# Moving elementwise work of a fast-multiplication MoE kernel: add and clamp in one VectorE operation, weight sums and half of the output accumulation to GpSimd and ScalarE

## The chip, the cores and the metric

The kernel runs on one core of one Trainium2 chip. The metric is the device time of one execution in microseconds (us). The engines are named as the profile names them: PE (TensorE matmul), PEld (its weight loads), DVE (VectorE), ACT (ScalarE), POOL (GpSimd) and SP (SyncE, which here only issues DMAs). All of them run their own instruction streams in order and meet through semaphores.

## The reference

A sparse attention (a window of 16 on either side, and summaries of blocks of 32 keys) gives `x`, 3072 rows of 512. A dense mixture of experts with Sinkhorn weights follows, which is where nearly all of the work lies:

```python
logits = x @ w_gate
P = np.exp(logits - logits.max())
for _ in range(8):
    P /= P.sum(1, keepdims=True) + 1e-09
    P /= P.sum(0, keepdims=True) + 1e-09
    P *= N / E
for e in range(E):                       # E = 8, N = 3072, D = 512, F = 1024
    h = np.maximum(x @ w1[e], 0.0)
    ye = h @ w2[e]
    out += P[:, e:e + 1] * ye
```

## The kernel before

**Stages.** The attention, the gate and all of expert 0 come first. Their units of work are put in order by a planner (class `Plan`), which has costs and dependencies for each unit; its course runs on through the transition (`bridge`), where the eight Sinkhorn steps run on DVE and POOL beside the last products of expert 0 and the first four groups of expert 1. From there on the order is written out by hand, in a loop over n. The last four steps are written out once more (`last`).

**Fast multiplication.** Experts 1 to 7 compute both products in seven block products instead of eight (Strassen's scheme in Winograd's form). Each of them needs sums and differences of blocks of both factors, and of the results. For the first product of a group these are `p1` to `p7`, for the second `q1` to `q7`.

**One iteration** of the loop handles one group (expert e, columns j of 512 rows, part i of the hidden units; 12 groups per expert, i innermost) of the first product, and the pair of output tiles `ta`, `tb` of the group four iterations earlier (LAG = 4) of the second product. PE runs, in this order: q1 (the end of the last line of the iteration before), p1, p5, q5, p6, p2, q6, p3, p7, q2, q4, q3, p4, q7. A p product is two matmuls of 512 columns, a q product four of 256. The other engines, in PSUM banks `pa`, `pb`, `pg` (first product) and `xy` (second product, two buffers of two banks):

- ACT: `r21` (relu of the group before), `c1` (copy of q1's result), `seed` (pa to pg), `c5` and `c2` (copies of pb and pg into SBUF), `r11` (relu), `v6` (a copy inside xy).
- DVE, before: `ya` and `yb` of the pair before (line 1125: out_acc = xy * P + out_acc, 512 elements each), `v5` (xy and c1 into xy, read by q6), `s4` of the group before, then `c12` and `c22` (line 933: pb + c2 and pg + c5 into the f16 tile hf), `r12` and `r22` (lines 1044 and 1047: the clamp at zero, in place), `s1`, `s3`, `s2` (lines 933 and 930: sums of the parts of hf, which the second product reads four iterations later). c22 must be over before p4 adds to the same bank pg, v5 before q6 adds to its part of xy.
- POOL, before: only DMA issues in this part of the kernel: `load_w1` and `load_w2`, which fetch the next expert's weights as f16. One w1 part's load follows each of the first three groups of j = 2, and waits until PE has used the buffer; w2 and the first part of w1 are loaded at j = 1, i = 1.

**Weight sums.** `w1_sums(e, i)` makes three new blocks and overwrites one (four operations of 256 f16 elements); `w2_sum(e, n)` makes one block of 1024 f16 elements. For experts 2 to 7 the loop places w1 parts 0 and 1 at j = 2, i = 2 and 3 of the expert before, w1 parts 2 and 3 at j = 0, i = 0 and 1, the first two w2 sums at j = 2, i = 0 and 1 of the expert before, and the last two at j = 0, i = 2 and 3. Those of expert 1 are in the transition, but for what the planner leaves open.

The lines of the loop that set this order around the change:

```python
            do("q1", "p1")
            do0("r21")
            do("c1", "seed")
            do0("ya", "yb")
            ...
            do("p2", "r11")
            do("q6", "v6")
            do("p3", "c12")
            do("p7", "c22", "r12")
            do("q2", "q4", "q3")
            do("r22", "s1", "s3", "p4", "s2", "q7")
            if groups[n - LAG][0] == 1:
                do("scale0")
```

`do` is for the group and pair of this iteration, `do0` for those of the one before. `scale0` scales expert 0's share of the two output tiles on ACT (line 1081), in expert 1 only. In the last expert each finished tile is stored by SP (line 1129), ta after `ya` and tb after `fin`.

Of the kernel before, what the change touches and what calls it, by code (L numbers as in the profile page):

```python
# [8 lines left out]

FP32 = mybir.dt.float32  # L10
BF16 = mybir.dt.bfloat16
FP16 = mybir.dt.float16
AF = mybir.ActivationFunctionType
ALU = mybir.AluOpType
# [20 lines left out]
class Plan:  # L35
# [13 lines left out]
    def add(self, eng, cost, fn, deps=(), prio=0.0, opens=(), uses=(), lag=0.0, shape=None):  # L49
        u = Unit(eng, cost, fn, [d for d in deps if d is not None], prio, list(opens), lag, shape)  # L50
        for b in list(opens) + list(uses):
            b.users.append(u)
        if uses and eng != "PE":
            u.prio -= 100.0
        self.waiting.append(u)
        return u
# [80 lines left out]
def kernel(  # L137
# [29 lines left out]
    ROW = PAD + HG * (LIVE + PAD) + W + PAD  # L167
    NEH = 3
    XS = 64.0

    const = ctx.enter_context(tc.tile_pool(name="const", bufs=1))
    persist = ctx.enter_context(tc.tile_pool(name="persist", bufs=1))
# [742 lines left out]
    if True:  # L915
# [10 lines left out]
        xTs = fast.tile([128, 3, KH, NH], FP16, name="xTs")  # L926
        ws1, ws2, hs = {}, {}, {}

        def sub(out, in0, in1):
            nc.vector.tensor_tensor(out=out, in0=in0, in1=in1, op=ALU.subtract)  # L930

        def plus(out, in0, in1):
            nc.vector.tensor_tensor(out=out, in0=in0, in1=in1, op=ALU.add)  # L933

        def moving1(what, j):
            t = slice(512 * j, 512 * (j + 1))
# [17 lines left out]
        def w1_sum(e, i, n):  # L954
            if n == 0:
                ws1[e, i] = fast.tile([128, 3, KH, 128], FP16, tag="ws1", name="ws1", bufs=5)
            m = {w: weight1(w, e, i) for w in "A11 A12 A21 A22 S1 S2 S3 S4".split()}
            f, o, a, b = ((plus, "S1", "A21", "A22"), (sub, "S2", "S1", "A11"), (sub, "S3", "A11", "A21"),
                          (sub, "S4", "A12", "S2"))[n]
            f(m[o], m[a], m[b])  # L960

        def w1_sums(e, i):
            for n in range(4):
# [9 lines left out]
        def w2_sum(e, n):  # L973
            if n == 0:
                ws2[e] = hpool.tile([128, 3, FH, DH], FP16, tag="h", name="ws2")
            m = {w: moving2(w, e) for w in "B11 B12 B21 B22 T1 T2 T3 T4".split()}
            sub(*[m[w] for w in (("T1", "B12", "B11"), ("T2", "B22", "T1"), ("T3", "B22", "B12"),
                                 ("T4", "T2", "B21"))[n]])

        def product1(e, i, j, bank, a, b, start):  # L980
            w, x = weight1(a, e, i), moving1(b, j)
# [10 lines left out]
        def group(e, j, i):  # L992
            h = hs[e, j, i] = fast.tile([128, 7, 512], FP16, tag="hf", name="hf", bufs=8)
            B = {}

            def p1():
                B["a"] = fps.tile([128, 512], FP32, tag="ab", name="pa", bufs=2)
                product1(e, i, j, B["a"], "A11", "B11", True)

            def seed():  # L1000
                B["g"] = fps.tile([128, 512], FP32, tag="g", name="pg", bufs=2)
                nc.scalar.copy(out=B["g"][:], in_=B["a"][:])  # L1002

            def p5():
                B["b"] = fps.tile([128, 512], FP32, tag="ab", name="pb", bufs=2)
                product1(e, i, j, B["b"], "S1", "T1", True)

            def c5():
                B["c5"] = fast.tile([128, 512], FP32, tag="c5", name="c5", bufs=1)
                nc.scalar.copy(out=B["c5"][:], in_=B["b"][:])  # L1010

            def p6():
                product1(e, i, j, B["g"], "S2", "T2", False)

            def c2():
                B["c2"] = fast.tile([128, 512], FP32, tag="c2", name="c2", bufs=1)
                nc.scalar.copy(out=B["c2"][:], in_=B["g"][:])  # L1017

            def p2():
                product1(e, i, j, B["a"], "A12", "B21", False)  # L1020

            def r11():
                relu("ACT", h[:, A11, :], B["a"][:])

            def p3():
                product1(e, i, j, B["b"], "S4", "B22", False)

            def c12():
                plus(h[:, A21, :], B["b"][:], B["c2"][:])

            def p7():
                product1(e, i, j, B["g"], "S3", "T3", False)

            def c22():
                plus(h[:, A22, :], B["g"][:], B["c5"][:])

            def p4():
                product1(e, i, j, B["g"], "A22", "T4", False)

            def r21():  # L1040
                relu("ACT", h[:, A12, :], B["g"][:])

            def r12():
                nc.vector.tensor_scalar_max(out=h[:, A21, :], in0=h[:, A21, :], scalar1=0.0)

            def r22():
                nc.vector.tensor_scalar_max(out=h[:, A22, :], in0=h[:, A22, :], scalar1=0.0)

            def s1():
                plus(h[:, S1, :], h[:, A21, :], h[:, A22, :])  # L1050

            def s3():
                sub(h[:, S3, :], h[:, A11, :], h[:, A21, :])

            def s2():
                sub(h[:, S2, :], h[:, S1, :], h[:, A11, :])

            def s4():
                sub(h[:, S4, :], h[:, A12, :], h[:, S2, :])

            return {f.__name__: f for f in (p1, seed, p5, c5, p6, c2, p2, r11, p3, c12, p7, c22, p4,
                                            r21, r12, r22, s1, s3, s2, s4)}

        def pair(e, j, c, spare=False, c1_at=None, tail=False):
            def h(q):
# [55 lines left out]
            def add(t, k, *src):  # L1121
                src = part(*src)
                w = src.shape[1]
                acc = out_acc[:, t, k * DH:(k + w) * DH].rearrange("p (h d) -> p h d", h=w)
                nc.vector.scalar_tensor_tensor(out=acc, in0=src, scalar=P_sb[:, t, e:e + 1], in1=acc,  # L1125
                                               op0=ALU.mult, op1=ALU.add)
# [2 lines left out]
                eng.dma_start(out=out[t * 128:(t + 1) * 128, k], in_=out_acc[:, t, k])  # L1129

            def ya():
                add(ta, 0, 0, 3)
                if e == E - 1:
                    store(ta)

# [34 lines left out]
        def bridge():  # L1170
# [54 lines left out]
            for i in range(4):  # L1225
                f = made[1, 0, i] = group(1, 0, i)
                a, b, g = Buffer("ab"), Buffer("ab"), Buffer("g")
                k5, k2 = Buffer("c5"), Buffer("c2")
                d = {}

                def op(name, eng, us, deps, opens=(), uses=()):
                    d[name] = add(eng, us, f[name], [d[x] if isinstance(x, str) else x for x in deps],
                                  1000.0 + PRI[i], opens=opens, uses=uses)

                op("p1", "PE", 0.44, [U["w1n", i]], [a])
                op("seed", "ACT", 0.58, ["p1"], [g], [a])
                op("p5", "PE", 0.44, ["p1", Wt[i, 0], X[0, 0]], [b])
                op("c5", "ACT", 0.58, ["p5"], [k5], [b])
                op("p2", "PE", 0.44, ["seed"], (), [a])
                op("r11", "ACT", 0.58, ["p2"], (), [a])  # L1240
                op("p6", "PE", 0.44, ["seed", Wt[i, 1], X[0, 1]], (), [g])
                op("c2", "ACT", 0.58, ["p6"], [k2], [g])
                op("p3", "PE", 0.44, ["c5", Wt[i, 3]], (), [b])
                op("c12", "DVE", 0.68, ["p3", "c2"], (), [b, k2])
                op("p7", "PE", 0.44, ["c2", X[0, 2]], (), [g])
                op("c22", "DVE", 0.68, ["p7", "c5"], (), [g, k5])
                op("p4", "PE", 0.44, ["c22", X[0, 3]], (), [g])
                op("r21", "ACT", 0.58, ["p4"], (), [g])
                op("r12", "DVE", 0.3, ["c12"])
                op("r22", "DVE", 0.3, ["c22"])  # L1250
                op("s1", "DVE", 0.42, ["r12", "r22"])
                op("s3", "DVE", 0.42, ["s1", "r11"])
                op("s2", "DVE", 0.42, ["s1"])
                op("s4", "DVE", 0.42, ["s2", "r21"])
# [7 lines left out]
                u.fn()  # L1262
        first.close()
        xps = ctx.enter_context(tc.tile_pool(name="xps", bufs=1, space=PSUM, side="right", reuse_waits="tile"))
        NOTHING = {}
        g = q = NOTHING
        for n in range(LAG, len(groups)):
# [6 lines left out]
            def do(*names):  # L1274
                for nm in names:
                    f = g.get(nm) or q.get(nm)
                    if f is not None:
                        f()

            def do0(*names):  # L1280
                for nm in names:
                    f = g0.get(nm) or q0.get(nm)
                    if f is not None:
                        f()
# [4 lines left out]
            do("q1", "p1")  # L1289
            do0("r21")  # L1290
            do("c1", "seed")
            do0("ya", "yb")
            do("p5", "c5")
            do("q5", "v5")
            do0("s4", "fin")
# [10 lines left out]
                w2_sum(e, i)  # L1306
            do("p2", "r11")
            do("q6", "v6")
            do("p3", "c12")
            do("p7", "c22", "r12")  # L1310
            do("q2", "q4", "q3")
            do("r22", "s1", "s3", "p4", "s2", "q7")
            if groups[n - LAG][0] == 1:
                do("scale0")
            if j == 2 and i < 3 and later:
# [54 lines left out]
```

## Time and profile before

| | |
|---|---|
| median of 3 runs | 669.99 us (669.78 to 670.46) |
| span of the profiled execution | 667.9 us |
| mean granted TensorE clock | 0.999 |
| c12 and c22, 84 times each (DVE) | 692 and 680 ns |
| r12 and r22, 84 times each (DVE) | 284 and 287 ns |
| ya and yb, 164 times together (DVE) | 744 ns |
| s1, s2, s3, s4 (DVE, 512 f16) | 425 ns |
| a copy of 256 or 512 elements from PSUM (ACT) | 372 and 585 ns |
| a scaled copy of 256 elements from PSUM (ACT, line 1152) | 474 ns |
| an f32 operation on two SBUF tensors on POOL: 192 elements (lines 1184 and 1201, medians) | 517 and 592 ns |
| the same, 256 elements (lines 1140 and 1158, in the tail) | 726 and 723 ns |
| a DMA issue of a w1 half part (POOL) | 758 ns |

The result's file has only times of the runs; the profiled execution's own time is not among them, and stands as its span. A busy share is of the span; an idle time that a row shows in brackets is that of the engine just before it, with what ended it. The end of a matmul is modelled, and neighbouring matmuls overlap in the rows.

### The profile page before, as it was taken

What the parts mean: (1) busy time and instruction counts of PE and PEld (TensorE: products, weight loads), DVE (VectorE), ACT (ScalarE), POOL (GpSimd) and SP (SyncE); (2) the same over time, 40 slices, a digit from 0 to 9 for tenths busy, and PEclk for the clock granted to TensorE, in tenths of its full rate; (3) what the DMA queues carried; (4) which work ended last, traced back from release to release, by engine and by line L of the source; (5) the groups of instructions that cost most, each with busy time, mean ns of one, the idle gap of its engine ahead of it and who ended that gap; (6) DMA issues with size and microseconds to landing.
All of it is one profiled execution on the core that took longest, in us unless ns stands there. A gap on an engine that the chain in (4) does not pass through costs nothing.

```text
span 667.9 us, 13518 instructions
## 1 busy us (share of the span) xinstructions
PE 659.0 (99%) x5077; PEld 435.7 (65%) x5077; DVE 582.2 (87%) x1475; ACT 399.7 (60%) x782; POOL 131.8 (20%) x179
## 2 busy tenths in 40 slices
PE   8999999999999999999999999999999999999996
PEld 4766656555666666666666666666666666666665
DVE  8889998785999988998799978998899889998885
ACT  6777676566777765555555555555555555555551
POOL 8699404223011010201010000101020101100001
PEclk9999999999999999999999999999999999999999
DMA  9999939500513050503231051306040233201224
GB/s 162 184 154 147 148 72 95 71 1 8 73 17 32 1 80 1 49 1 55 26 33 17 0 80 17 33 1 79 1 47 3 39 41 29 20 1 64 79 80 158
DMA packets 124033, 36.75 MB, mean 55 GB/s; under 512 B 110144, under 2 KB 121152, under 8 KB 123968
## 3 DMA queue, kind: packets, MB, share of 16 engines
q0 software_dynamic: 104128, 25.93, 41.2%
q1 hardware_dynamic: 18880, 9.22, 6.1%
q8 instruction: 40, 0.66, 0.4%
q10 hardware_dynamic: 960, 0.74, 0.3%
q14 instruction: 25, 0.20, 0.1%
HBM read 52.45 MB, written 6.29 MB: 88 GB/s over the span
## 4 chain that ended last, share of the span: by engine, by line
PE 89%; DVE 7%; DMA 1%; ACT 1%; issue 1%; ACTq 0%; DVEq 0%
PE xy L989 37%; PE pg L983 16%; PE pa L983 11%; PE pb L983 11%; PE yps L231 5%; PE hps L221 5%; DVE xs L547 1%; DMA kT<-kst 1%; PE sg L383 1%; PE tkq L349 1%; DVE em L435 1%; DVE km L377 1%; DVE h L214 0%; DVE kh L375 0%; PE tx L554 0%
## 5 line engine op out<-in xcount | busy, mean ns | idle before, releaser
L989 PEld LDWEIGHTS <-hf 128*128 128x128 f16 x2352 | 230.1, 98 | 95.8 <-issue 0.8
L989 PE MATMUL xy<-w,hf 128*128 128x256 f16 x1312 | 183.4, 273 | 0.0
L989 PE MATMUL xy<-ws,hf 128*128 128x256 f16 x984 | 147.6, 273 | 0.1
L212 ACT ACTIVATE hf<-pg 128x512 f16<-128x512 f32 x84 | 50.1, 597 | 151.3 <-PE pg L983 151.2
L1125 DVE SCALAR_TENSOR_TENSOR out_acc<-xy,P_sb,out_acc 128x512 f32<-128x512 f32 x164 | 115.1, 744 | 2.1 <-PE xy L989 2.1
L930 DVE TENSOR_TENSOR hf<-hf 128x512 f16<-128x512 f16 x252 | 100.3, 425 | 8.9 <-DVE hf L933 0.5
L983 PE MATMUL pa<-xT,w 128*128 128x512 f16 x336 | 99.9, 379 | 0.0
L983 PEld LDWEIGHTS <-w 128*128 128x128 f16 x672 | 65.8, 98 | 43.5
L933 DVE TENSOR_TENSOR hf<-pb,c 128x512 f16<-128x512 f32 x84 | 58.1, 692 | 36.7 <-PE pb L983 34.4
L197 POOL DMA_DIRECT2D w<-in_moe_w_dram x56 | 41.8, 758 | 219.9 <-PE pg L983 191.7
L983 PEld LDWEIGHTS <-ws 128*128 128x128 f16 x504 | 49.3, 98 | 25.1
L1017 ACT COPY c<-pg 128x512 f32<-128x512 f32 x84 | 49.2, 585 | 22.4 <-PE pg L983 22.4
L933 DVE TENSOR_TENSOR hf<-pg,c 128x512 f16<-128x512 f32 x84 | 57.1, 680 | 0.7 <-PE pg L983 0.7
L212 ACT ACTIVATE hf<-pa 128x512 f16<-128x512 f32 x84 | 50.6, 603 | 0.9 <-PE pa L983 0.9
L1002 ACT COPY pg<-pa 128x512 f32<-128x512 f32 x84 | 47.9, 570 | 4.9
L983 PE MATMUL pg<-xT,w 128*128 128x512 f16 x168 | 50.0, 379 | 0.0
L983 PE MATMUL pg<-xTs,w 128*128 128x512 f16 x168 | 50.0, 379 | 0.0
L983 PE MATMUL pb<-xTs,ws 128*128 128x512 f16 x168 | 50.0, 379 | 0.0
L983 PE MATMUL pb<-xT,ws 128*128 128x512 f16 x168 | 50.0, 379 | 0.0
L983 PE MATMUL pg<-xTs,ws 128*128 128x512 f16 x168 | 50.0, 379 | 0.0
L1010 ACT COPY c<-pb 128x512 f32<-128x512 f32 x84 | 49.8, 593 | 0.0
L221 PE MATMUL hps<-xT,w 128*128 128x384 f16 x256 | 48.9, 326 | 0.0
(152 smaller groups left out, 827.5 us busy)
## 6 DMA issues: line engine op xcount, KB each, us to landing
w<-in_moe_w_dram POOLq DMA_DIRECT2D x8, 1024.0 KB, 9.0
w<-in_moe_w_dram POOLq DMA_DIRECT2D x56, 128.0 KB, 3.5
out_dram<-out_acc SPq DMA_DIRECT2D x20, 256.0 KB, 2.0
vx<-in_v_dram POOLq DMA_DIRECT2D x16, 192.0 KB, 5.9
qst<-in_q_dram POOLq DMA_DIRECT2D x31, 96.0 KB, 5.2
kst<-in_k_dram POOLq DMA_DIRECT2D x24, 96.0 KB, 5.4
w<-in_moe_w_dram POOLq DMA_DIRECT2D x2, 512.0 KB, 8.8
Ve<-vx SPq DMA_DIRECT2D x48, 10.2 KB, 4.0
```

The source lines that it names most:

```text
L197: nc.gpsimd.dma_start(out=t[:, :, h, :], in_=moe_w1[e].rearrange("(dk p) f -> p dk f", p=128)[:, :, f:f + 128])
L212: nc.scalar.activation(out=out, in_=in_, func=AF.Relu, bias=0.0, scale=1.0)
L221: nc.tensor.matmul(hp[:, 0:n], lhsT=w1s[e][:, dk, 128 * f:128 * (f + 1)], rhs=xT[:, dk, t0:t0 + n], start=(dk == 0), stop=(dk == KD - 1))
L231: nc.tensor.matmul(yp[:], lhsT=h[:, f, c * 128:(c + 1) * 128], rhs=w2s[e][:, f, :], start=(f == 0), stop=(f == KF - 1))
L930: nc.vector.tensor_tensor(out=out, in0=in0, in1=in1, op=ALU.subtract)
L933: nc.vector.tensor_tensor(out=out, in0=in0, in1=in1, op=ALU.add)
L983: nc.tensor.matmul(bank[:], lhsT=w[:, dk, :], rhs=x[:, dk, :], start=start and dk == 0, stop=dk == KH - 1, skip_group_check=True)
L989: nc.tensor.matmul(bank, lhsT=a(f)[:, 128 * c:128 * (c + 1)], rhs=w[:, f, :], start=start and f == 0, stop=f == FH - 1, skip_group_check=True)
L1002: nc.scalar.copy(out=B["g"][:], in_=B["a"][:])
L1010: nc.scalar.copy(out=B["c5"][:], in_=B["b"][:])
L1017: nc.scalar.copy(out=B["c2"][:], in_=B["g"][:])
L1125: nc.vector.scalar_tensor_tensor(out=acc, in0=src, scalar=P_sb[:, t, e:e + 1], in1=acc, op0=ALU.mult, op1=ALU.add)
```

## The change

Three edits, and what they pull with them:

1. `c12` and `c22` become one custom DVE operation each (`relu_plus`: add, upper bound at the largest float, lower bound at zero). `r12` and `r22` are gone, from the planner's units too.
2. `w1_sum` and `w2_sum` of experts 2 to 7 run on POOL.
3. `ya` of the loop's pairs is split: ACT makes a scaled copy of both halves of the xy bank pair into an SBUF tile `ys` (two buffers, a new pool), POOL adds it to `out_acc`. It stands behind `v6` of the next iteration, where it stood at that iteration's start before. The four pairs of the tail keep the old form.

```diff
+        def relu_plus(out, in0, in1):
+            nc.vector._custom_dve(TENSOR_ADD_SAT, out=out, in0=in0, in1=in1, s0=FLT_MAX, s1=0.0)
...
-            f(m[o], m[a], m[b])
+            f(m[o], m[a], m[b], nc.vector if e == 1 else nc.gpsimd)
...
-                                 ("T4", "T2", "B21"))[n]])
+                                 ("T4", "T2", "B21"))[n]], nc.vector if e == 1 else nc.gpsimd)
...
-                plus(h[:, A21, :], B["b"][:], B["c2"][:])
+                relu_plus(h[:, A21, :], B["b"][:], B["c2"][:])
...
-                plus(h[:, A22, :], B["g"][:], B["c5"][:])
+                relu_plus(h[:, A22, :], B["g"][:], B["c5"][:])
...
-            def r12():
-                nc.vector.tensor_scalar_max(out=h[:, A21, :], in0=h[:, A21, :], scalar1=0.0)
-
-            def r22():
-                nc.vector.tensor_scalar_max(out=h[:, A22, :], in0=h[:, A22, :], scalar1=0.0)
...
             def ya():
-                add(ta, 0, 0, 3)
+                if tail:
+                    add(ta, 0, 0, 3)
+                else:
+                    y = late.tile([128, 2, DH], FP32, tag="ys", name="ys", bufs=2)
+                    nc.scalar.activation(out=y[:], in_=part(0, 3), func=AF.Copy, scale=P_sb[:, ta, e:e + 1])
+                    acc = out_acc[:, ta, :].rearrange("p (h d) -> p h d", h=2)
+                    nc.gpsimd.tensor_tensor(out=acc, in0=acc, in1=y[:], op=ALU.add)
...
-                op("r12", "DVE", 0.3, ["c12"])
-                op("r22", "DVE", 0.3, ["c22"])
-                op("s1", "DVE", 0.42, ["r12", "r22"])
+                op("s1", "DVE", 0.42, ["c12", "c22"])
...
-            do0("ya", "yb")
+            do0("yb")
...
             do("q6", "v6")
+            do0("ya")
             do("p3", "c12")
-            do("p7", "c22", "r12")
+            do("p7", "c22")
             do("q2", "q4", "q3")
-            do("r22", "s1", "s3", "p4", "s2", "q7")
+            do("s1", "s3", "p4", "s2", "q7")
```

`sub` and `plus` got an argument for the engine. In the loop PE's instructions keep their order; in the transition the planner puts one four-matmul part of expert 0's last products (yps) and the small Sinkhorn totals a few places later or earlier.

## The prediction

> **What bounds the kernel now.** The page first: each engine's share, then the time by stage.
>
> ```profile
> PE 659.0 (99%) x5077; PEld 435.7 (65%) x5077; DVE 582.2 (87%) x1475; ACT 399.7 (60%) x782; POOL 131.8 (20%) x179
> ```
>
> ```profile
> 100.00:140.00 40.00, 39.80 (x320) 22.90 (x319) 32.24 (x96) 23.97 (x47) 13.03 (x20) 1.00 0.64 70
> 250.00:300.00 50.00, 50.00 (x347) 33.72 (x345) 45.79 (x110) 28.35 (x59) 4.48 (x6) 1.00 0.17 17
> 650.00:668.00 18.00, 12.37 (x111) 10.52 (x108) 10.09 (x21) 3.70 (x11) 2.82 (x4) 0.95 0.40 147
> ```
>
> In the second view the columns after each window are its length, then PE, PEld, DVE, ACT, POOL, granted clock and DMA. From 140 to 650 us PE has no idle time, at a full granted clock, and the chain of waits shows one iteration every 6.08 us, 80 of them. 14 products of 512 columns and 28 of 256 (14336 columns) in 6.08 us leave PE nothing to gain there. A change on the other engines can win only the 8.9 us in which PE is idle, nearly all at the two ends, and can lose in every iteration. So the question is the slack of each result PE waits for. One iteration, with p1 at 406.82 called 0 from here on:
>
> ```profile
> 404.05 0.69 DVE L933 TENSOR_TENSOR hf<-pb,c 128x512 f16<-128x512 f32 x1 [0.97 <-PE pb L983]
> ...
> 404.65 0.68 DVE L933 TENSOR_TENSOR hf<-pg,c 128x512 f16<-128x512 f32 x1
> ...
> 407.68 0.60 PE L989 MATMUL xy<-ws,hf 128*128 128x256 f16 x4
> ...
> 408.39 0.43 DVE L933 TENSOR_TENSOR xy<-xy,c 128x256 f32<-128x256 f32 x1
> ...
> 408.98 0.60 PE L989 MATMUL xy<-ws,hf 128*128 128x256 f16 x4
> ...
> 409.78 0.39 ACT L1107 COPY xy<-xy 128x256 f32<-128x256 f32 x1
> ...
> 411.59 0.59 PE L983 MATMUL pg<-xTs,w 128*128 128x512 f16 x2
> ...
> 412.38 0.76 DVE L930 TENSOR_TENSOR hf<-hf 128x512 f16<-128x512 f16 x2
> ```
>
> Two DVE results are tight. v5 starts at 1.57, 0.11 after q5's end, ends at 2.00, and q6 takes it at 2.16; with a hop of about 0.06 (ACT's c1 in the tail ends at 653.17, the weight load it releases is at 653.23) the slack is 0.10 us. c12 and c22 run 3.30 to 4.59 (404.05 and 404.65 are those of the iteration before, which began at 400.74) and p4 takes c22's release at 4.77: slack 0.12. All else on DVE (ya, yb, s1, s3, s2, s4) is needed much later, but stands ahead of these two in DVE's order.
>
> The third view is the one stage where POOL computes beside DVE (the Sinkhorn steps):
>
> ```profile
> 130.98 0.59 POOL L1201 TENSOR_TENSOR P_sb<-P_sb,crec_sb 128x192 f32<-128x192 f32 x1 [3.65 <-DVE crec_sb L1196]
> 131.16 1.03 DVE L930 TENSOR_TENSOR hf<-hf 128x512 f16<-128x512 f16 x2
> ...
> 145.00 0.64 DVE L933 TENSOR_TENSOR hf<-pg,c 128x512 f16<-128x512 f32 x1
> 145.22 0.59 POOL L1201 TENSOR_TENSOR P_sb<-P_sb,crec_sb 128x192 f32<-128x192 f32 x1 [2.90 <-DVE crec_sb L1196]
> ...
> 150.11 0.86 POOL L1201 TENSOR_TENSOR P_sb<-P_sb,crec_sb 128x192 f32<-128x192 f32 x1 [2.88 <-DVE crec_sb L1196]
> 150.44 1.08 DVE L930 TENSOR_TENSOR w<-w 128x1024 f16<-128x1024 f16 x1
> ...
> 155.86 1.65 DVE L930 TENSOR_TENSOR hf<-hf 128x512 f16<-128x512 f16 x3
> ...
> 156.08 0.62 POOL L1201 TENSOR_TENSOR P_sb<-P_sb,crec_sb 128x192 f32<-128x192 f32 x1 [3.06 <-DVE crec_sb L1196]
> ```
>
> The pair s3, s2 takes 0.76 alone and 1.03 here, the 1024-element subtraction 0.68 alone and 1.08 here, and POOL's own operation 0.59 alone and 0.86. A DVE operation with one operand in PSUM (145.00) costs and suffers nothing. Both delays are the overlap less 0.14 us: 131.57-131.16-0.14 = 0.27, 150.97-150.44-0.14 = 0.39. So a DVE operation on two SBUF tensors stands still until POOL's is over, and the other way round.
>
> **A rule against the change.** The Trainium skill, "SBUF — State Buffer", section "Who interferes with whom", says that a DVE instruction with two SBUF inputs and a GpSimd instruction that reads SBUF exclude each other for a whole instruction, the later one waiting. The rows agree with it (0.27 and 0.39 lost). Were the path shared at half rate, those losses would be about 0.2 and 0.27, and the sum below would be near zero instead of +32.
>
> **The change, part by part.** Durations are of the profiled execution: span 667.9 us, with some 2.1 us around it against the median 669.99.
>
> *Fused add and clamp.* 84 times c12 and c22 become a custom add-min-max; r12 and r22 (168 at 0.285 us, 48 us of DVE) go. They lay beside PE, so nothing is won but earlier s1, s3, s2. The trace has no such operation. Below: 0.63, the shortest plain add of this shape. Above: 0.74, the row with two operations in one pass (out_acc, 744 ns). I take 0.69, same operands. At 0.74 c22 ends 0.11 later, within the slack of 0.12: no cost at either end.
>
> *ya to ACT and POOL.* 80 operations of 0.744 leave DVE. ACT takes a scaled copy: 0.474 for 256 from PSUM with scale, plain copies of 256 and 512 differ by 0.22, so 0.70. It stands behind v6 (2.96 to 3.35) and runs 3.25 to 3.95, in ACT's gap of 2.06 us before r21 at 5.41; in expert 1 the two scale0 (0.722 each) follow and still end by 5.3. xy is needed by the q1 after next, some 1.9 us later. POOL's add comes next. POOL's prices: 192 elements 0.59, 256 elements 0.723, so 2.1 ns each, 512: 1.26, 1024: 2.3. Steeper (from 0.517 for 192): 1.54 and 3.2; gentler, if f16 goes at twice the rate as it does on DVE: 1024 in 1.2, 256 in 0.36. I take the first, from the two shapes nearest. The add holds 4.0 to 5.26. s1, now ready at 4.63, waits for it, so s1, s3, s2 end near 6.5, yb (due 6.24, 0.70 long) follows, and v5 at 7.65 is not late: no cost by itself. SP's store of ta falls behind that of tb in the last expert, some 4 us later; the last one moved is issued before 655, and the span ends at 667.9. POOL's issue of the w1 loads stands behind the add; they have an iteration to spare.
>
> *Weight sums on POOL, 6 experts.* DVE loses per expert 16 x 0.285 + 4 x 0.685 = 7.3 us, which lay beside PE: nothing won. POOL gains, per expert, 16 of 0.72 and 4 of 2.3: 11.5 + 9.2, with 12 adds (15.1) and ten load issues of 0.76 to 0.9 (8) some 44 of the 73 us of twelve iterations, so it keeps up. The trace has no f16 arithmetic on POOL; the bounds above cover it. But POOL runs a sum as soon as it is free, which is right behind the add, not where the program has it. There: s1 gets through at 5.26 to 5.58, POOL's waiting sum goes next, at 5.55.
> - w2 sum (2.3): until 7.85; s3 and s2 end 8.47, yb runs from 8.4, v5 starts 9.15 instead of 7.65. Less 0.10: PE stalls 1.4 us.
> - w1 sums (4 x 0.72) alternate with s3 and s2: 6.27, s3 to 6.6, next sum to 7.27, s2 to 7.6, yb, v5 at 8.23: PE stalls 0.48.
> - Where a w1 load's issue (1.48, after p4) stands between, the sum starts near 6.95, behind s2; it meets only s4, and c12 is about 0.12 late: nothing.
>
> Without a load ahead are, per expert, three w2 sums (the two of j=0 and the first of j=2) and two w1 blocks (both of j=0): 18 x 1.4 + 12 x 0.48 = 25.2 + 5.8 = 31, and with roundings 32. 670.0 + 32 = **702 us**. By the gentler prices w2 stalls 0.4 and w1 not: 677. By the steeper, 2.5 and 0.75, and the sums behind a load cost 0.9: 670 + 45 + 9 + 5 = 729.
>
> *Order in the transition and the tail.* Without r12 and r22 the planner moves some yps products; PE idles 0.2 us there: 0.3 either way. In the tail PE waits 0.24 and 0.29 for c1; ACT's ya (0.70) now stands ahead of the second c1: 0.5 less to 0.3 more. I take nothing.
>
> **Rivals.**
> - *All is absorbed, 670* (0.17). DVE and POOL share instead of excluding, or s1, s3, s2 go before POOL's next operation. For it: with s3 and s2 at half rate s2 ends 6.9, v5 at 7.6, on time. Against: the 0.39, and at 155.86 a POOL operation came in between three DVE operations.
> - *The custom operation is slow* (0.08). From 0.06 us more each, the excess counts twice in 84 groups; at 0.2 more, (0.4-0.12) x 84 = 23.5, so 693 without the port and about 725 with it. Against: it moves the same elements through the same operands.
> - *POOL falls behind* (0.09). Were a w1 sum 1.3, four, an add and waits for DVE (5 x 0.3) need 8.0 of 6.08 us; ACT's ya then waits for a ys buffer, with r21 and the next seed behind it: 1.9 in four iterations of six experts, 46 in place of the 5.8: 670 + 26 + 46 = 742. Against: it needs almost twice the row of 0.723.
> - *Faster* (0.04). PE's idle time before 140 us and in the tail (0.83 and 0.53) is waited out for DVE, and the shorter DVE work takes all of it: 670.0-1.36 = 668.6. It decides only if no iteration loses 0.02 us.
>
> **How the numbers follow.** The forecast has 0.62, on its own 677 to 729. The range goes down into the absorbed case, 669.5, and up to 732: left out are most of the backlog and of the faster case. Below 0.2% (1.34 us), about what can be told from no change: 0.17; slower 0.62+0.08+0.09 = 0.79; faster 0.04.
>
> **What would show it.** Iterations with a sum right behind an add stretch by 1.4 or 0.5 us, with PE idle at q6 for v5; the others stay 6.08. The s operations show long durations under POOL's, c12 and c22 stay 0.69, POOL's 1024 takes 2.3. Wrong if PE stays without idle time, if idle time falls at p4 (custom operation, or s4 held), or if POOL's prices differ.

## The result, and the profile after

The changed kernel takes 689.76 us (median of 4 runs, 689.28 to 690.50) against 669.99: ratio 1.029, 95% interval 1.0277 to 1.0302. It is 19.8 us slower. The forecast was 702 with a range of 669.5 to 732: right in sign and mechanism, too high by 12 us (19.8 us lost, where 32 were forecast). The profiled execution has a span of 687.6 us, 19.7 more than that of before.

The page of the changed kernel, busy time and share of each engine, and the groups that matter:

```profile
PE 663.4 (96%) x5077; PEld 435.4 (63%) x5077; DVE 541.9 (79%) x1108; ACT 449.2 (65%) x861; POOL 357.6 (52%) x379
...
L1137 POOL TENSOR_TENSOR out_acc<-out_acc,ys 128x512 f32<-128x512 f32 x80 | 101.5, 1269 | 229.4 <-ACT ys L1135 229.4
...
L994 PE MATMUL xy<-ws,hf 128*128 128x256 f16 x984 | 147.5, 272 | 14.7 <-DVE xy L935 14.5
L932 DVE TENSOR_TENSOR hf<-hf 128x512 f16<-128x512 f16 x252 | 149.3, 618 | 9.9 <-ACT hf L214 1.6
...
L938 DVE CUSTOM_DVE_ANT_0 hf<-pb,c 128x512 f16<-128x512 f32 x84 | 58.0, 690 | 66.8 <-PE pb L988 60.8
...
L935 DVE TENSOR_TENSOR hf<-hf 128x512 f16<-128x512 f16 x84 | 70.6, 841 | 2.9
...
L1135 ACT ACTIVATE ys<-xy,P_sb 128x512 f32<-128x512 f32 x80 | 55.7, 696 | 0.0
```

Of the kernel before, the rows of the `xy<-ws,hf` products, of s2, s3 and s4, and of s1:

```profile
L989 PE MATMUL xy<-ws,hf 128*128 128x256 f16 x984 | 147.6, 273 | 0.1
L930 DVE TENSOR_TENSOR hf<-hf 128x512 f16<-128x512 f16 x252 | 100.3, 425 | 8.9 <-DVE hf L933 0.5
L933 DVE TENSOR_TENSOR hf<-hf 128x512 f16<-128x512 f16 x84 | 35.6, 424 | 2.8
```

DVE is less busy than before (542 for 582 us), and yet PE now waits for it: 14.5 us in front of the `xy<-ws,hf` products, for line 935 (v5). The s operations, the same instructions as before, went from 425 ns to 618 (s2, s3, s4, line 932) and from 424 to 841 (s1, line 935). The custom operation costs what the plain add cost (690 and 692 ns). The stages, in the same columns as before:

```profile
250.00:300.00 50.00, 49.08 (x339) 32.96 (x337) 39.61 (x66) 32.25 (x64) 30.85 (x33) 1.00 0.30 34
300.00:350.00 50.00, 47.69 (x329) 31.96 (x328) 39.11 (x63) 31.08 (x62) 22.31 (x17) 1.00 0.24 30
```

The clock is granted in full (1.00), so the time is lost in waits. The starts of p1 say in which iterations: the first of the hand-written loop starts 0.33 us later than before, the last 18.93 later, so the loop has 18.60 of the 19.7 us, the transition 0.33 and what follows the last p1 0.74.

| iteration | how many | longer than 6.08 us by |
|---|---|---|
| first w2 sum (j = 2, i = 0 of the expert before) | 6 | 0.99 to 1.06 |
| third w2 sum (j = 0, i = 2) | 6 | 0.98 to 1.00 |
| fourth w2 sum (j = 0, i = 3) | 6 | 0.80 |
| second w2 sum, behind a load (j = 2, i = 1) | 6 | 0.05, once 0.64 |
| w1 sums of j = 0, i = 0 | 6 | up to 0.13, once 0.24 |
| w1 sums of j = 0, i = 1; those behind a load | 18 | under 0.02, once 0.25 |

(The single values of 0.24 and 0.25 have in them a late start of a VectorE operation, which the last section tells of.) The 18 iterations with a w2 sum right behind an add hold 16.8 of the 18.6 us. One of them, by engine; its p1 starts at 188.33, and the iteration that starts at 182.25 is shown from its c12 on:

```profile
185.59 0.69 DVE L938 CUSTOM_DVE_ANT_0 hf<-pb,c 128x512 f16<-128x512 f32 x1 [0.41 <-PE pb L988]
186.20 0.68 DVE L938 CUSTOM_DVE_ANT_0 hf<-pg,c 128x512 f16<-128x512 f32 x1
186.91 0.94 DVE L935 TENSOR_TENSOR hf<-hf 128x512 f16<-128x512 f16 x1
187.95 2.49 DVE L932 TENSOR_TENSOR hf<-hf 128x512 f16<-128x512 f16 x2
190.37 0.74 DVE L1124 SCALAR_TENSOR_TENSOR out_acc<-xy,P_sb,out_acc 128x512 f32<-128x512 f32 x1
191.03 0.42 DVE L935 TENSOR_TENSOR xy<-xy,c 128x256 f32<-128x256 f32 x1
```

```profile
186.29 1.28 POOL L1137 TENSOR_TENSOR out_acc<-out_acc,ys 128x512 f32<-128x512 f32 x1 [4.80 <-ACT ys L1135]
187.52 2.31 POOL L932 TENSOR_TENSOR ws<-w 128x1024 f16<-128x1024 f16 x1
```

```profile
190.06 0.59 PE L988 MATMUL pa<-xT,w 128*128 128x512 f16 x2
191.50 0.60 PE L994 MATMUL xy<-ws,hf 128*128 128x256 f16 x4 [0.84 <-DVE xy L935]
```

c12 and c22, each with one operand in PSUM, keep their lengths, though POOL's add begins during c22 (186.29). s1 waits for the end of the add (187.57): 0.94 in place of 0.42. The pair s3, s2 waits for the end of the w2 sum (189.83): 2.49 in place of 0.76. By the rule from the trace of before, the delays should be the overlap less 0.14: 187.57-186.91-0.14 = 0.52 and 189.83-187.95-0.14 = 1.74; they are 0.52 and 1.73. yb and v5 themselves run at full speed but late, and q6 starts 1.01 us behind its place.

### The profile page after: what moved, and what is told of

It is laid out like the page before. It is cut to its first block, busy times and chain, and to the rows that moved or that the text cites. A ratio compares the mean times of both kernels' runs of the same rounds, so it can differ in the third digit from the quotient of the medians.

```text
span 687.6 us, 13410 instructions
## 1 busy us (share of the span) xinstructions
PE 663.4 (96%) x5077; PEld 435.4 (63%) x5077; DVE 541.9 (79%) x1108; ACT 449.2 (65%) x861; POOL 357.6 (52%) x379
## 4 chain that ended last, share of the span: by engine, by line
PE 75%; DVE 20%; DMA 2%; issue 2%; ACT 1%; DVEq 0%; ACTq 0%
PE xy L994 31%; PE pg L988 13%; PE pb L988 10%; PE pa L988 8%; DVE hf L932 5%; PE yps L233 5%; PE hps L223 5%; DVE hf L938 3%; DVE out_acc L1124 2%; DVE hf L935 2%; DVE xs L549 1%; DVE xy L935 1%; DMA kT<-kst 1%; DMA vx<-in_v_dram 1%; PE sg L385 1%
## 5 line engine op out<-in xcount | busy, mean ns | idle before, releaser
L1137 POOL TENSOR_TENSOR out_acc<-out_acc,ys 128x512 f32<-128x512 f32 x80 | 101.5, 1269 | 229.4 <-ACT ys L1135 229.4
L994 PE MATMUL xy<-ws,hf 128*128 128x256 f16 x984 | 147.5, 272 | 14.7 <-DVE xy L935 14.5
L932 DVE TENSOR_TENSOR hf<-hf 128x512 f16<-128x512 f16 x252 | 149.3, 618 | 9.9 <-ACT hf L214 1.6
L938 DVE CUSTOM_DVE_ANT_0 hf<-pb,c 128x512 f16<-128x512 f32 x84 | 58.0, 690 | 66.8 <-PE pb L988 60.8
L935 DVE TENSOR_TENSOR hf<-hf 128x512 f16<-128x512 f16 x84 | 70.6, 841 | 2.9
L1124 DVE SCALAR_TENSOR_TENSOR out_acc<-xy,P_sb,out_acc 128x512 f32<-128x512 f32 x84 | 62.3, 743 | 3.0 <-PE xy L994 2.1
L935 DVE TENSOR_TENSOR xy<-xy,c 128x256 f32<-128x256 f32 x82 | 35.1, 428 | 33.5 <-PE xy L994 33.3
L938 DVE CUSTOM_DVE_ANT_0 hf<-pg,c 128x512 f16<-128x512 f32 x84 | 57.1, 680 | 0.7 <-PE pg L988 0.7
L1135 ACT ACTIVATE ys<-xy,P_sb 128x512 f32<-128x512 f32 x80 | 55.7, 696 | 0.0
```

What stands on the lines that cost most here:

```text
L932: eng.tensor_tensor(out=out, in0=in0, in1=in1, op=ALU.subtract)
L935: eng.tensor_tensor(out=out, in0=in0, in1=in1, op=ALU.add)
L938: nc.vector._custom_dve(TENSOR_ADD_SAT, out=out, in0=in0, in1=in1, s0=FLT_MAX, s1=0.0)
L994: nc.tensor.matmul(bank, lhsT=a(f)[:, 128 * c:128 * (c + 1)], rhs=w[:, f, :], start=start and f == 0, stop=f == FH - 1, skip_group_check=True)
L1135: nc.scalar.activation(out=y[:], in_=part(0, 3), func=AF.Copy, scale=P_sb[:, ta, e:e + 1])
L1137: nc.gpsimd.tensor_tensor(out=acc, in0=acc, in1=y[:], op=ALU.add)
```

## The experiments

The theory: all of the loss is DVE operations on two SBUF tensors standing still while POOL reads SBUF, and it reaches PE only where a sum follows the add at once (A). The rivals: the custom operation (B), the longer way of ya (C), a sum of many small shares (D), the amount of POOL's work or traffic wherever it lies (E). Each ratio is to runs of the kernel before on the same chip, with its 95% interval.

**One part at a time.** The first three kernels start from the kernel before and make one edit each of the list under "The change": the first (fused add and clamp), the third (ya split) and the second (weight sums). The fourth is the changed kernel without its weight sums on POOL:

```diff
-            f(m[o], m[a], m[b], nc.vector if e == 1 else nc.gpsimd)
+            f(m[o], m[a], m[b])
...
-                                 ("T4", "T2", "B21"))[n]], nc.vector if e == 1 else nc.gpsimd)
+                                 ("T4", "T2", "B21"))[n]])
```

> The kernel before with only the fused add and clamp; weight sums and ya stay on VectorE. Theory A (the whole loss is VectorE operations on two SBUF tensors standing still while GpSimd works): nothing runs on GpSimd in the loop, so every iteration stays 6.08 us and the time is 670.0 +- 0.7. Theory B (the custom operation or its release of p4 costs something in each iteration): the loss shows here, up to 690, with idle time of PE before p4.

> The kernel before with only ya split into ScalarE's copy and GpSimd's add. Theory A: GpSimd's add (1.27 us, 4.04 to 5.3 in the iteration) holds up s1, which without the fusion is ready at 5.03, by 0.3 us; s2 ends near 6.6, yb near 7.3, v5 is still on time at 7.65: 670 to 671, iterations of 6.08. Theory C (the longer way of ya holds its xy buffer or ScalarE, and PE waits): a good part of the 20 us, with idle time of PE before q1.

> The kernel before with only the weight sums of experts 2 to 7 on GpSimd; no fusion, ya on VectorE. Theory A: ya and yb on VectorE leave v5 no room (they end at 1.57, just when v5 is due), so each sum that falls on s1, s3, s2 costs PE its full length: some 3 to 4.5 us per expert, 688 to 697, so no less than the whole change. Theory D (the parts add up, and the sums are only some of the loss): clearly under 689, 675 to 685.

> The whole change without its weight sums, which stay on VectorE. Theory A: every iteration has one GpSimd add that holds s1 from 4.63 to 5.3, and nothing behind it; s2 ends near 6.5: no wait of PE, 670 to 671. Theories B and C: 680 to 690, since custom operation, ScalarE copy and GpSimd add are all in.

| kernel | median, us | ratio |
|---|---|---|
| fused only | 670.45 | 1.0007 (0.9998 to 1.0016) |
| ya split only | 671.07 | 1.0014 (1.0004 to 1.0024) |
| sums on POOL only | 699.85 | 1.0442 (1.0414 to 1.0470) |
| fused and split | 671.34 | 1.0018 (1.0009 to 1.0028) |

B and C fall: what they name costs nothing or about 1 us. The sums alone lose 29.7 us, more than the whole change, since with ya and yb both on DVE there is no room left between s2 and v5. That was expected, though the measured time is above the 688 to 697 that stood for it. Nor is the time lost where the whole change loses it: of 28.3 us in the loop, 17.2 fall in the iterations of j = 0, i = 1, 5.7 in those of i = 0 and 4.4 in those of j = 1, i = 2. Without an add to wait for in each iteration, POOL runs ahead of the loop's order: in the first such stretch it does the w1 sums of j = 0 and both w2 sums of j = 0 in one row, from 210.36 to 220.73. So the edits don't add up: the other two soften what the sums do. One thing in this trace was not expected; r12 and r22 (lines 1049 and 1052 here), which the fusion takes away, have only one operand:

```profile
217.86 0.89 DVE L1049 TENSOR_SCALAR hf<-hf 128x512 f16<-128x512 f16 x1
218.67 2.21 DVE L1052 TENSOR_SCALAR hf<-hf 128x512 f16<-128x512 f16 x1
```

```profile
216.48 2.12 POOL L932 TENSOR_TENSOR w<-w 128x1024 f16<-128x1024 f16 x1
218.57 2.16 POOL L932 TENSOR_TENSOR ws<-ws,w 128x1024 f16<-128x1024 f16 x1
```

The clamps, 0.28 us alone, stand still as well, until POOL's operations end at 218.60 and 220.73. The Trainium skill, "SBUF — State Buffer", section "Who interferes with whom", has this too: a one-input operation that runs in a mode with two ports takes the shared path. The 2.21 us agree with it; which mode the clamp ran in, no trace shows.

**The same sums, later.** A copy of one element, which needs s2's result, keeps POOL from starting a block of sums before s2 is done:

```diff
+            if (j == 2 and later or e > 1 and j == 0):
+                nc.gpsimd.tensor_copy(out=held2[0:1, 0:1], in_=hs[groups[n - 1]][0:1, S2, 0:1])
             if j == 2 and i > 1 and later:
                 w1_sums(e + 1, i - 2)
```

> The whole change, with one tiny GpSimd copy (one element of s2's output) ahead of each block of weight sums, so that a sum can't start until s1, s3 and s2 are done. GpSimd does the same work and a little more; only its place within the iteration moves by 1.3 us. Theory A: a w2 sum then runs about 6.8 to 9.1 and meets only s4, c12 stays in time or is 0.1 late: 670.5 to 673. Theory E (it is GpSimd's amount of work, or its traffic to SBUF beside PE, wherever it lies): stays near 690.

> The kernel with only the weight sums on GpSimd (699.9), with the tiny GpSimd copy of one element of s2's output ahead of each block. Theory A: the sums start after s2 (6.3 in the iteration) instead of on top of r22, s1, s3 and s2, and run beside ya, yb and v5, which have one operand in PSUM; only s4 waits: 670 to 673. If ya's place on VectorE leaves too little room whatever the sums do: 685 or more.

The whole change with held sums takes 672.49 us (1.0038, 1.0023 to 1.0052), the sums alone with the same hold 671.15 (1.0016, 1.0006 to 1.0025), for 699.85 without. POOL does as many sums as in the changed kernel and a little more, and nearly all of the loss is gone, so E falls. (Of the 2.5 us that are left, the fused and split kernel has 1.2 as well; the rest lies in the iterations of j = 2, i = 1, 0.12 each and once 0.72.) An iteration with a w2 sum in the first of the two (POOL, then DVE):

```profile
231.42 0.18 POOL L1305 COPY held<-hf 1x1 f16<-1x1 f16 x1 [1.28 <-DVE hf L932]
231.56 2.12 POOL L932 TENSOR_TENSOR ws<-ws,w 128x1024 f16<-128x1024 f16 x1
```

```profile
230.52 0.76 DVE L932 TENSOR_TENSOR hf<-hf 128x512 f16<-128x512 f16 x2
231.20 0.74 DVE L1124 SCALAR_TENSOR_TENSOR out_acc<-xy,P_sb,out_acc 128x512 f32<-128x512 f32 x1
232.47 0.43 DVE L935 TENSOR_TENSOR xy<-xy,c 128x256 f32<-128x256 f32 x1 [0.53 <-PE xy L994]
232.82 1.15 DVE L932 TENSOR_TENSOR hf<-hf 128x512 f16<-128x512 f16 x1
234.27 0.69 DVE L938 CUSTOM_DVE_ANT_0 hf<-pb,c 128x512 f16<-128x512 f32 x1 [0.30 <-ACT xy L1106]
```

v5 again waits for PE, not PE for v5. Only s4 stands still (1.15), and c12 behind it has 0.30 us to spare.

**Which sums.** The whole change, with the w1 sums back on DVE, and, in the second kernel, the w2 sums in the same way:

```diff
-            f(m[o], m[a], m[b], nc.vector if e == 1 else nc.gpsimd)
+            f(m[o], m[a], m[b])
```

> The whole change, with the w1 sums left on VectorE; only the w2 sums (24 of 2.3 us) are on GpSimd. From the trace of the changed kernel an iteration with a w2 sum right behind the add is 1.0, 1.0 and 0.8 us longer, the fourth 0.05: 6 x 2.85 = 17 us, so 687 +- 1.5. If it goes by GpSimd's busy time, w2 has 54 of the 127 us that the sums take: 670 + 0.43 x 19 = 678.

> The whole change, with the w2 sums left on VectorE; only the w1 sums (96 of 0.76 us) are on GpSimd. Alternating with s1, s3, s2, they cost PE 0.07 to 0.24 us per block right behind an add: 12 blocks, 1 to 3 us, so 671.5 to 673.5. If it goes by GpSimd's busy time: 670 + 0.57 x 19 = 681.

With only the w2 sums on POOL: 688.30 us (1.0274, 1.0259 to 1.0289). With only the w1 sums: 672.08 (1.0029, 1.0018 to 1.0041), of which the fused and split kernel without any sums on POOL has 671.34. Both as expected from the lengths of the iterations, and neither by POOL's busy time: 24 long operations lose 17 us, 96 short ones under 1.

**Reads or any work.** Two kernels without any sum on POOL, but with an operation on a spare tile, which nobody reads, at the places of the w2 sums; the output is unaffected:

```diff
+        spare = late.tile([128, 2, 1024], FP16, name="spare")
...
+            if j == 2 and i < 2 and later or e > 1 and j == 0 and i > 1:
+                nc.gpsimd.memset(spare[:, :, :], 0.0)
```

```diff
+            if j == 2 and i < 2 and later or e > 1 and j == 0 and i > 1:
+                nc.gpsimd.tensor_tensor(out=spare[:, 0, :], in0=spare[:, 0, :], in1=spare[:, 1, :], op=ALU.add)
```

> The fused and split kernel with all weight sums on VectorE, and at each of the 24 places of a w2 sum one GpSimd fill of a spare tile (2048 f16 elements) that reads nothing and whose result nobody uses. Theory A in its narrow form (VectorE waits for GpSimd's reads of SBUF): no wait of PE, 670 to 671. Theory A in its wide form (any GpSimd operation on SBUF): as much as its length allows, up to 17 us.

> The same as the kernel with the extra GpSimd fills (fused, split, all weight sums on VectorE, 24 places), but the extra GpSimd operation is an add of two 1024-element f16 rows of a spare tile that nobody uses: about the length of a w2 sum (2.3 us, the fill took 1.81), with two reads of SBUF. It has no connection to any data of the kernel. Narrow theory A (reads block VectorE's two-operand work): iterations of 7.0 as in the changed kernel, 686 to 690. If the loss came from the sums' data or semaphores: 671.

The fill: 671.31 us (1.0022, 1.0013 to 1.0032), as without it (671.34). The add: 694.11 (1.0364, 1.0346 to 1.0381). The POOL and DVE rows of the same iteration, first with the fill, then with the add:

```profile
186.98 1.81 POOL L1314 MEMSET spare<- 128x2048 f16 x1
```

```profile
187.43 0.76 DVE L932 TENSOR_TENSOR hf<-hf 128x512 f16<-128x512 f16 x2
```

```profile
187.41 2.30 POOL L1314 TENSOR_TENSOR spare<-spare 128x1024 f16<-128x1024 f16 x1
```

```profile
187.83 2.49 DVE L932 TENSOR_TENSOR hf<-hf 128x512 f16<-128x512 f16 x2
```

Beside a fill that writes for 1.81 us, s3 and s2 run at full speed; beside an add that reads, they lose 1.73. No data of the kernel passes through the spare tile, so neither the sums' data nor their semaphores are the cause. The Trainium skill, "SBUF — State Buffer", section "Who interferes with whom", says just this, that such a DVE instruction contends with a GpSimd instruction that reads SBUF and not with one that only writes; the 0.76 and 2.49 agree. The add costs more than the sums did (694 for 690; 686 to 690 was expected), because DVE now makes the w2 sums too: the iteration behind a load, 0.05 longer in the changed kernel, is 0.65 longer here, as such a sum (0.68) stands between s4 and c12 and p4 waits for c22.

**The rest.** Fused and split, 1.2 us remain. The split kernels' traces show a wait in the tail, so the last `ya` before it was put back in the old form:

```diff
-                      (A, "c1"), (q, "ya"), (q, "yb"),
+                      (A, "c1"), (q, "ya_whole"), (q, "yb"),
```

> The fused and split kernel without weight sums on GpSimd (671.3), but the last pair before the tail has its ya in the old form on VectorE. In the trace of the split kernel yb waits 0.87 us for ScalarE's scaled copy there, s4 and v5 follow late, and PE waits 0.59 for v5. If that is the rest of the loss, 670.4 to 670.7; if the rest is spread over the loop, 671.3.

It takes 671.23 us (1.0019, 1.0010 to 1.0028), not to be told apart from 671.34. The wait of PE for v5 (0.6 us) is gone from the trace; but POOL's small operations of the tail now fall on s3 and s2 (1.29 for 0.76), and the time behind the last p1 is 24.32 us, for 24.60 in the fused and split kernel and 23.89 before. The tail of that kernel costs some 0.7 us, then, and this experiment won back little of it. No kernel of this study is faster than the one before; the fused one alone is not told apart from it.

## Why the prediction was right, and where its sizes were off

| step of the prediction | forecast | measured |
|---|---|---|
| custom add-min-max | 0.69 us | 0.690 and 0.680 |
| ACT's scaled copy of 512 | 0.70 | 0.696 |
| POOL's add of 512, begin and end in the iteration | 1.26; 4.0 to 5.26 | 1.27; 4.04 to 5.32 |
| w2 sum, 1024 f16 | 2.3 | 2.31 beside DVE, 2.12 when held |
| w1 sum, 256 f16 | 0.72 | 0.66 to 0.96, mean 0.76 |
| stall, w2 sum right behind the add | 18 x 1.4 = 25.2 | 12 x 1.0 + 6 x 0.8 = 16.8 |
| stall, w1 sums right behind the add | 12 x 0.48 = 5.8 | about 0.5 in all |
| behind a load | 0 | 0.9 in all |
| transition and tail | 0 (0.3 either way; -0.5 to +0.3) | +0.33 and +0.74 |

- **The size.** The forecast of 31 us in the loop stands against 18.6; the 1.1 us outside it, forecast as nothing, bring the measured loss up to 19.7. The 0.33 of the transition can't be told from none: the loop's first p1 starts 0.55 us later than before in the fused and split kernel, and 0.19 earlier in the same kernel with fills.
- **What bounds the kernel, and the slack.** Right: with the sums away nothing of the change is seen in the loop's waits. v5 is the tight result, and its slack of 0.10 is confirmed within 0.02: v5 started 8.78 after p1 instead of 7.65, 1.13 late, and q6 was 1.01 late.
- **The price of standing still.** Right, to 0.01 us, in the rows shown above.
- **Where POOL's next operation falls.** This is the term that was mis-sized. The prediction let s1 run to its end first and then charged the sum in full, 5.55 to 7.85, as if a price of 2.3 had no waiting in it. In fact POOL issues the sum as the add ends (187.52, 5.27 in the iteration), and its 2.31 us include the wait for s1; alone, when held, it takes 2.12. It ends at 7.58. That the price of 2.3, drawn from f32 rows, meets the recorded 2.31 is luck. The 0.27 us, and 0.1 from the spacing of yb and v5, are the difference of 1.4 and 1.0. In a following w2 iteration POOL's add begins some 0.2 earlier against the delayed PE, hence the 0.8.
- **The w1 sums.** The same term, four times: s3 and s2 slip in between sums that are issued back to back, and the pair takes 1.51 us (219.40 in the changed kernel) where the working had 2.0. s2 ends 7.21 after p1 instead of 7.6, and v5 is 0.13 to 0.20 late where nothing else holds it, of which 0.10 is slack. So 0.48 shrank to less than 0.1 in ten of the twelve.
- **Sums behind a load.** Right, but for one of six: there, the load's issue waited 0.6 longer for PE, and the sum behind it held s4 and through it c12 and c22, by 0.5 us for p4.
- **The tail.** The step failed: it allowed 0.3 us more at most. There yb waits for ACT's scaled copy (0.87 us in the fused and split kernel), then POOL's add falls on s4; v5 is late by 0.6. The prediction had looked at ACT's queue only.
- **The rivals.** That all is absorbed: shared at half rate, s3 and s2 would have taken 1.5, not 2.49. That the custom operation is slow: 690 ns. That POOL falls behind: a w1 sum takes 0.96 at most, not 1.3. Faster: the loop lost in every expert.

## What to carry to other kernels

Freeing a busy engine wins nothing where another one has no idle time, as PE here; what counts is the slack of each result that the bound engine takes, here 0.1 us. Elementwise work moved to GpSimd is not beside VectorE's two-operand SBUF work but in turn with it, and its price is what stands behind the waiting instruction in VectorE's order: the same sums cost 30 us, 18 us or about 1, by where within an iteration they start and what stands behind them there. A one-element copy that needs the right result puts them there for 0.18 us.

## What the runs showed of the hardware that had not been expected

- A one-operand clamp on SBUF (f16, 512 elements, 0.28 us) stands still behind GpSimd as the two-operand ones do (0.89 and 2.21 us); a GpSimd fill, which only writes, holds up nobody.
- GpSimd adds f16 hardly faster than f32: 1024 f16 elements take 2.12 us and 256 take 0.66 when nothing is in the way, 1.9 ns for each further element; 512 in f32 take 1.27, where the line between the two f16 sizes gives 1.15 (an estimate). A fill of 2048 f16 elements takes 1.81.
- In single iterations PE loses 0.2 to 0.3 us that no POOL operation explains: four in the loop of the fused kernel and four in that of the fused and split one (0.8 us more in the loop, by its p1 starts), and one of 0.14 in the loop before. The wait is not PE's own: in each of the eight, c12, v5 or ACT's copy into c2 starts 0.28 to 0.37 us late, though the trace's semaphore wait in front of it ends at its usual time. The fused and split kernel has the four at the same places with the fills and with the old tail, the fused one at others. In all eight iterations the trace also has a packet of the DMA queue q14, which the page lists as "instruction"; 20 other iterations of these two kernels have one and are no longer than 6.08 us. Whether the packet and the late start have one cause was not tried. Together with the tail these waits are about the size of the 1 us that the split kernels lose.
